# Convolution and GELU feed-forward on one core: five buffers for convolved blocks, first taps on ScalarE, new instruction orders

## The chip, the core and the metric

The kernel runs on one NeuronCore of a Trainium2 chip. The core has five engines with an instruction stream each: TensorE (PE: matmuls; its weight loads are listed as PEld), VectorE (DVE), ScalarE (ACT), GpSimd (POOL) and SyncE (SP), which here only issues DMA transfers. The streams run in their own order and meet in semaphores. The metric is the device time of one execution in microseconds, the median of several runs.

## What is computed

x has 8 sequences of 4096 tokens with 192 features, in eight heads of 24. Each head has seven convolution weights, which are put through a softmax; the convolution is causal (six zeros ahead of each sequence). Its result goes through a feed-forward layer with 2048 hidden units and the exact GELU.

```python
def _attn_ref(x, weight):
    w = weight - np.max(weight, axis=-1, keepdims=True)
    w = np.exp(w)
    w = w / (np.sum(w, axis=-1, keepdims=True) + 1e-09)
    x_pad = np.concatenate([np.zeros((B, K - 1, D)), x], axis=1)
    x_unf = x_pad[:, idx, :].reshape(B, S, K, H, group)
    out = np.einsum('hk,bskhg->bshg', w, x_unf)
    ...
def _moe_ref(x, w_in, w_out):
    h = x @ w_in
    g = 0.5 * h * (1.0 + erf(h * inv_sqrt2))
    return g @ w_out
```

## The kernel before, in words

**Blocks.** The 32768 tokens are cut into two halves of 16384, which lie on the upper and lower 64 partitions. A half is cut into 35 blocks: blocks 0 to 5 of 256 tokens, blocks 6 to 34 of 512 (`WS`). For each block n:

- SyncE loads x into one of three `xin` buffers (`load`, L778; load n waits until block n-3 has been transposed).
- VectorE transposes it into `xT` (t*n* in the lists; L984), and GpSimd copies the six tokens ahead of it (`halo`, L892).
- The convolution has seven taps. The first (`k` = 0 in `tap`, L332) is a multiplication into `acc`; it can be done by VectorE (L340) or, third by third, by ScalarE (`first_tap`, L1118, L1123; written f0.n, f1.n, f2.n). Taps 1 to 6 multiply and add (L345), on VectorE; the last writes the convolved block in bf16 to `xc` (two buffers). Blocks 0 and 1 are convolved by TensorE.
- TensorE multiplies `xc` by w_in (`mm1`, L1258) in 16 slots of 12 matmuls (8 slots in the small blocks); each slot fills one of two PSUM buffers `hp`, which ScalarE empties by a GELU into `gT` (L1165).
- In the same slots TensorE does the second product, mm2, of the block before, so "TensorE's block n" is mm1(n) with mm2(n-1).

**N and S blocks.** For blocks 6 to 33, mm2 comes in two forms. N blocks multiply all of gT (`mm2_t`, L1343). The 18 S blocks (`ST`, L73) use a scheme of the Strassen kind (`mm2_s`, L1392), with fewer matmuls and more additions. VectorE (`st_add`) and the DMA engines (`st_dma`, accumulating transfers issued by GpSimd) form sums of gT: S1, S3, Dn, S4, in pieces such as S1.0.30 (piece 0 of block 30). Each piece must be there before the matmuls that use it. Behind the matmuls, ScalarE copies results out of four PSUM banks (`st_copy`, L743: p15, e, u, p3). GpSimd moves the copy u from the lower to the upper 64 partitions by two DMA transfers (cu into `uu`, cg into `gs`). VectorE combines them (`st_post`: k0 L751, k3 L758, k4 L764) and transposes the results into `osb` (ev.0, ev.1, ev.2; L776, for N blocks L463). k4 waits for cg, k3 for cu. k4, ev.2 and the copies also release PSUM banks to the next block's mm2. SyncE stores `osb` (L806).

**What sets the order.** It is written out by hand for four engines. `LIST[n]` is VectorE's: t is a transposition, a digit is a tap of block n, the rest are sums, k steps, transpositions to osb and, in the new version, w (a step of preparing the weights for mm2) and evac (emptying block 5). Blocks up to 8 have a default order, with w and evac at places given by `SIDE` (L570). `SLOT[n]` is ScalarE's: "5:f1.10" is an operation ahead of the GELU of slot 5 of block n. `GLIST` (L819) is GpSimd's. SyncE's loop (L1468) issues loads up to block n+4, or n+5 from block 8 on, and then store n-1. Every stream is strictly in order; an instruction that waits holds up all behind it.

Of the kernel before, what the change touches and what calls it, by code (L numbers as in the profile page):

```python
# [5 lines left out]
ALU = mybir.AluOpType  # L6
# [5 lines left out]
def bass_lightweight_conv__then__act_gelu_exact_kernel(  # L12
# [39 lines left out]
    NX = 3  # L52

# [22 lines left out]
        9: "ev.0.6 t10 1 2 ev.2.6 ev.1.6 3 4 5 6",  # L76
        10: "1 2 S1.0.8 t11 ev.0.7 3 4 S1.1.8 S1.2.8 ev.1.7 S3.2.8 5 6",
        11: "ev.2.7 Dn.1.8 S4.0.8 S4.1.8 k0.0.8 t12 1 2 3 ev.2.8 4 5 6",
        12: "t13 1 2 k4.0.8 S1.0.10 3 ev.0.9 4 ev.0.8 S1.1.10 k3.0.8 ev.1.8 5 ev.2.9 ev.1.9 S1.2.10 6",
        13: "Dn.1.10 S3.2.10 1 S4.0.10 S4.1.10 2 k0.0.10 S1.0.11 3 4 5 ev.2.10 S1.1.11 Dn.0.11 S1.2.11 Dn.1.11 S3.2.11 t14 6",  # L80
        14: "k4.0.10 0 S4.0.11 S4.1.11 k0.0.11 t15 k3.0.10 1 2 ev.2.11 ev.1.10 ev.0.10 3 4 5 6",
        15: "t16 1 2 S1.0.13 3 ev.0.12 k4.0.11 k3.0.11 S1.1.13 4 ev.1.11 5 ev.0.11 ev.1.12 S1.2.13 6",
        16: "S3.2.13 t17 ev.2.12 Dn.1.13 S4.0.13 S4.1.13 k0.0.13 S1.0.14 1 2 3 ev.2.13 S1.1.14 4 S1.2.14 5 S3.2.14 Dn.0.14 k4.0.13 Dn.1.14 S4.0.14 S4.1.14 k0.0.14 6",
        17: "ev.0.13 0 1 k3.0.13 ev.1.13 2 ev.2.14 3 t18 4 5 6",
        18: "k3.0.14 t19 S1.0.16 1 k4.0.14 2 ev.0.15 3 S1.1.16 4 ev.1.14 ev.0.14 S1.2.16 ev.1.15 ev.2.15 Dn.1.16 S3.2.16 5 6",
        19: "S4.0.16 k0.0.16 S4.1.16 S1.0.17 t20 1 S1.1.17 2 ev.2.16 Dn.0.17 S1.2.17 3 S3.2.17 4 Dn.1.17 k4.0.16 S4.0.17 S4.1.17 5 k0.0.17 k3.0.16 6",
        20: "0 t21 1 ev.2.17 2 ev.0.16 ev.1.16 3 4 k4.0.17 5 k3.0.17 ev.0.17 6",
        21: "S1.0.19 1 ev.0.18 2 t22 S1.1.19 3 ev.1.17 ev.2.18 S1.2.19 ev.1.18 4 Dn.1.19 S3.2.19 5 S4.0.19 S4.1.19 6",
        22: "k0.0.19 S1.0.20 t23 1 2 ev.2.19 S1.1.20 Dn.0.20 S1.2.20 3 S3.2.20 S4.0.20 Dn.1.20 k4.0.19 4 S4.1.20 ev.0.19 k0.0.20 5 6",
        23: "t24 0 k3.0.19 ev.1.19 ev.2.20 1 2 3 4 5 6",  # L90
        24: "t25 S1.0.22 k4.0.20 1 ev.0.21 2 S1.1.22 3 ev.1.21 ev.2.21 S1.2.22 S4.0.22 S3.2.22 k3.0.20 4 Dn.1.22 ev.0.20 ev.1.20 S4.1.22 5 k0.0.22 6",
        25: "1 t26 2 ev.2.22 3 4 5 6",
        26: "1 2 t27 S1.0.24 ev.0.23 3 k4.0.22 S1.1.24 4 k3.0.22 ev.0.22 ev.1.22 ev.1.23 S1.2.24 S3.2.24 5 ev.2.23 6",
        27: "S4.0.24 Dn.1.24 1 S4.1.24 k0.0.24 S1.0.25 t28 2 3 ev.2.24 S1.1.25 4 S1.2.25 Dn.0.25 Dn.1.25 S3.2.25 S4.0.25 k4.0.24 ev.0.24 k3.0.24 5 S4.1.25 k0.0.25 6",
        28: "t29 0 1 ev.1.24 ev.2.25 2 3 4 5 6",
        29: "t30 1 S1.0.27 ev.0.26 k3.0.25 2 S1.1.27 k4.0.25 3 4 S1.2.27 S3.2.27 ev.1.26 ev.1.25 ev.2.26 ev.0.25 S4.0.27 5 Dn.1.27 S4.1.27 6",
        30: "k0.0.27 t31 1 2 3 ev.2.27 4 5 6",
        31: "1 t32 2 k4.0.27 3 k3.0.27 S1.0.29 ev.1.27 ev.0.28 S1.1.29 4 5 ev.1.28 S1.2.29 6",
        32: "ev.0.27 Dn.1.29 S4.0.29 S3.2.29 ev.2.28 1 S4.1.29 2 k0.0.29 S1.0.30 3 t33 4 ev.2.29 Dn.0.30 S1.1.30 S1.2.30 5 6",
        33: "S3.2.30 k3.0.29 k4.0.29 Dn.1.30 S4.0.30 S4.1.30 ev.1.29 ev.0.29 k0.0.30 1 S1.0.31 2 ev.2.30 S1.1.31 3 S1.2.31 t34 S3.2.31 Dn.0.31 4 k4.0.30 Dn.1.31 S4.0.31 S4.1.31 k3.0.30 k0.0.31 5 6",  # L100
        34: "S1.0.32 S1.1.32 1 ev.2.31 ev.0.30 S1.2.32 Dn.0.32 S4.0.32 Dn.1.32 ev.1.30 S3.2.32 k4.0.31 S4.1.32 2 3 k0.0.32 4 5 S1.0.33 k3.0.31 6",
        35: "ev.2.32 S1.1.33 S1.2.33 Dn.0.33 S4.0.33 Dn.1.33 S3.2.33 ev.0.31 ev.1.31 k4.0.32 k3.0.32 ev.0.32 S4.1.33 k0.0.33 ev.1.32 ev.2.33 k4.0.33 ev.0.33 k3.0.33 ev.1.33",
    }
    SLOT = {
        7: "2:f0.9 3:f1.9 5:f2.9",
        8: "3:f0.10 3:f1.10 6:f2.10 13:f0.11",
        9: "5:f1.11 6:p15.8 10:f2.11 13:f0.12 14:e.8",
        10: "0:f1.12 2:u.8 3:p3.8 4:f2.12 6:f0.13 10:f1.13",
        11: "1:f2.13 6:p15.10 13:e.10",
        12: "0:p3.10 2:u.10 6:p15.11 8:f2.14 11:f0.15 13:e.11 14:f1.15",  # L110
        13: "1:p3.11 2:u.11 4:f2.15 11:f0.16",
        14: "1:f1.16 4:f2.16 6:p15.13 9:f2.17 14:e.13",
        15: "0:p3.13 2:u.13 6:p15.14 13:e.14",
        16: "0:u.14 2:p3.14 4:f0.18 6:f1.18 8:f2.18 10:f0.19 13:f1.19",
        17: "7:p15.16 10:f2.19 12:f2.20 14:e.16",
        18: "0:p3.16 2:u.16 6:p15.17 13:e.17",
        19: "0:u.17 2:f0.21 4:p3.17 6:f1.21 8:f2.21",
        20: "5:f0.22 6:p15.19 10:f1.22 10:f2.22 13:e.19 14:f2.23",
        21: "0:p3.19 2:u.19 6:p15.20 13:e.20 15:f0.24",
        22: "2:u.20 4:p3.20 5:f1.24 8:f2.24 11:f0.25",  # L120
        23: "5:f1.25 6:p15.22 10:f2.25 13:e.22 14:f0.26",
        24: "0:u.22 2:p3.22 4:f1.26 4:f2.26 12:f0.27",
        25: "1:f1.27 4:f2.27 6:p15.24 14:e.24",
        26: "0:p3.24 2:u.24 6:p15.25 11:f2.28 13:f0.29 14:e.25",
        27: "0:p3.25 2:f1.29 4:u.25 6:f2.29",
        28: "0:f0.30 2:f1.30 6:p15.27 10:f2.30 13:f0.31 14:e.27",
        29: "0:f1.31 2:f2.31 3:u.27 4:p3.27 8:f0.32 10:f1.32 13:f2.32",
        30: "6:p15.29 14:e.29",
        31: "0:p3.29 2:u.29 4:f0.33 7:p15.30 8:f1.33 9:f2.33 13:e.30",
        32: "0:p3.30 2:u.30 4:f0.34 7:p15.31 9:f1.34 10:f2.34 15:e.31",  # L130
        33: "0:p3.31 2:u.31 6:p15.32 13:e.32",
        34: "0:p3.32 2:u.32 7:p15.33 15:e.33 15:u.33",
# [3 lines left out]
    AT1 = {4: (3, 5, 6), 5: (3, 5, 6), 6: (2, 3, 5)}  # L136
    for n in range(M0 + 3, NB):
        AT1[n] = [(b, i) for b in SLOT for i, k, m in SLOT[b] if k[0] == "f" and m == n]
# [51 lines left out]
    with es:  # L190
# [17 lines left out]
        xc = [sbt("xc%d" % i, [128, NP * TB], BF16) for i in range(2)]  # L208
# [5 lines left out]
        sst = {k: sbt("s_" + k, [128, NF // 2 * TB], BF16) for k in ("S1", "Dn", "S4")}  # L214
        gsm = sbt("gsm", [128, TB], F32)
        p5s = sbt("p5s", [128, TB], F32)
        uu = sbt("uu", [128, TB], F32)
        tq = sbt("tq", [128, TB], F32)
# [45 lines left out]
        S_AD = {k: sem("S_AD" + k) for k in ("S3.0", "S3.1", "S3.2", "Dn.0", "Dn.1", "cp.0", "cp.1", "cu", "cg")}  # L264
# [35 lines left out]
        def conv_out(e, n, j):  # L300
            kd, h, d0, dw = pieces(n)[j]
            p, ex, c0, w = kinds(n)[kd]
            e.wait_ge(S_PC, PCB[n] + kd + 1)
            ro = slice(0, 128) if h is None else slice(64 * h, 64 * h + 64)
            ri = ro if not ex else slice(64 - 64 * h, 128 - 64 * h)
            o = p * TB + c0 + d0
            dst = xc[n % 2][ro, o : o + dw]
            cb = 512 * cbank(n, kd) + d0
            src = ob[ri, cb : cb + dw]
            if (n == 0 and j in PA) or (n, j) == (1, 0):  # L310
                e.activation(out=dst, in_=src, func=AF.Copy).then_inc(S_PCA)
            else:
                e.tensor_copy(dst, src).then_inc(S_PCE)
# [18 lines left out]
        def tap(e, n, k, p0, pn):  # L332
# [9 lines left out]
            if k == KS - 1:  # L342
                dst = ap(xc[n % 2], p0 * TB, [[NP * TB, 128], [TB, pn], [1, w]])
                e.wait_ge(S_MM1, SL0[n - 1])
# [213 lines left out]
        for m in ST:  # L558
            for name in SUMS:
                for q in range(len(SUMS[name]) - 1):  # L560
                    p = "%s.%d" % (name, q)
                    key, one = (p, 16) if p in BYDMA[m] else (name, 1)
                    count[key] = count.get(key, 0) + one
# [947 lines left out]
```

## Time and profile before

| | us |
|---|---|
| median of 3 runs (667.45, 668.77, 668.36) | 668.36 |
| time of the profiled execution | 666.53 |
| its span, first to last instruction | 664.8 |
| VectorE busy | 623.6 |
| of it the convolution's taps 1 to 6 (L345) | 339.0 |
| ScalarE busy | 591.1 |
| of it the GELUs (L1165) | 514.6 |
| of it first taps (L1123), 77 of them | 53.5 |
| GpSimd busy | 105.5 |

The span is one execution, taken by the hardware profiler; what lies around it is 1.7 us. "Busy" is the time in which an engine executes an instruction. A wait row names the engine that waited, the operation it waited with, the engine and operation that ended the wait, the total, the number of times and the longest. In the rows of instruction groups there stand the line, engine, operation, output and input, count, busy time, mean in ns, and the idle time of the engine just ahead of them.

### The profile page before, as it was taken

What the parts mean: (1) busy time and instruction counts of PE and PEld (TensorE: products, weight loads), DVE (VectorE), ACT (ScalarE), POOL (GpSimd) and SP (SyncE); (2) the same over time, 40 slices, a digit from 0 to 9 for tenths busy, and PEclk for the clock granted to TensorE, in tenths of its full rate; (3) what the DMA queues carried; (4) which work ended last, traced back from release to release, by engine and by line L of the source; (5) the groups of instructions that cost most, each with busy time, mean ns of one, the idle gap of its engine ahead of it and who ended that gap; (6) DMA issues with size and microseconds to landing.
All of it is one profiled execution on the core that took longest, in us unless ns stands there. A gap on an engine that the chain in (4) does not pass through costs nothing.

```text
span 664.8 us, 27970 instructions
## 1 busy us (share of the span) xinstructions
PE 658.9 (99%) x12792; PEld 478.9 (72%) x12792; DVE 623.6 (94%) x564; ACT 591.1 (89%) x691; POOL 105.5 (16%) x175
## 2 busy tenths in 40 slices
PE   9999999999999999999999999999999999999997
PEld 8999655576776677778777666757666757677776
DVE  5989999999999999999999999999999999999962
ACT  8899988898899898989889998989898998999882
POOL 8000540102010110202120102110102030111010
DMA  9746675645914691596189145959245838352454
GB/s 156 162 96 133 109 121 122 136 98 130 216 40 113 156 193 34 138 206 124 38 192 221 34 106 120 195 115 225 45 98 136 184 82 192 66 113 50 92 134 112
DMA packets 146438, 83.66 MB, mean 126 GB/s; under 512 B 129936, under 2 KB 138192, under 8 KB 146320
## 3 DMA queue, kind: packets, MB, share of 16 engines
q1 hardware_dynamic: 129328, 49.42, 33.7%
q0 software_dynamic: 15872, 31.86, 23.7%
q8 instruction: 100, 1.64, 1.0%
q10 hardware_dynamic: 1120, 0.59, 0.3%
q14 instruction: 18, 0.15, 0.1%
HBM read 31.51 MB, written 25.17 MB: 85 GB/s over the span
## 4 chain that ended last, share of the span: by engine, by line
PE 94%; DMA 2%; DVE 2%; POOL 1%; issue 1%; ACT 0%; DVEq 0%; POOLq 0%; ACTq 0%
PE hp L1258 48%; PE ob L1392 25%; PE ob L1343 16%; PE ob L1298 4%; DVE acc L345 1%; PE hp L1448 1%; DMA win<-in_moe_w_in_dram 1%; DMA xin<-in_x_dram 1%; PE ob L1448 1%; DMA uu<-uu 0%; ACT gT L1165 0%; POOL win L839 0%; DVE xT L984 0%; POOL xTb L360 0%; DVE xc L345 0%
## 5 line engine op out<-in xcount | busy, mean ns | idle before, releaser
L1165 ACT ACTIVATE gT<-hp 128x1024 bf16<-128x1024 f32 x510 | 514.6, 1022 | 60.1 <-PE hp L1258 52.7
L1258 PE MATMUL hp<-xc,win 64*64 64x512 bf16 (+2 forms) x6036 | 432.6, 366 | 0.5 <-DVE xc L345 0.4
L1258 PEld LDWEIGHTS hp<-xc,win 64*64 64x64 bf16 (+1 forms) x6036 | 229.1, 105 | 88.6 <-ACT gT L1165 5.9
L345 DVE SCALAR_TENSOR_TENSOR acc<-xT,wcol,acc 128x1536 f32<-128x1536 f32 (+1 forms) x165 | 282.3, 1711 | 7.4 <-ACT acc L1123 4.6
L1392 PE MATMUL ob<-gT,wot 64*64 64x512 bf16 x1152 | 219.6, 376 | 0.0
L1392 PE MATMUL ob<-gT,wst 64*64 64x512 bf16 (+2 forms) x1152 | 203.1, 323 | 0.7 <-DVE p5s L764 0.7
L1343 PE MATMUL ob<-gT,wot 64*64 64x512 bf16 x1920 | 133.5, 376 | 0.0
L1392 PE MATMUL ob<-s_S,wot 64*64 64x128 bf16 (+2 forms) x864 | 132.5, 305 | 0.0
L1392 PEld LDWEIGHTS ob<-gT,wst 64*64 64x64 bf16 x1152 | 98.5, 107 | 16.3 <-DVE p5s L764 1.6
L1392 PEld LDWEIGHTS ob<-gT,wot 64*64 64x64 bf16 x1152 | 89.5, 107 | 10.9 <-DVE osb L776 0.5
L1343 PEld LDWEIGHTS ob<-gT,wot 64*64 64x64 bf16 x1920 | 63.9, 107 | 39.7 <-DVE osb L776 0.3
L1392 PEld LDWEIGHTS ob<-s_S,wot 64*64 64x64 bf16 x864 | 68.6, 107 | 15.9
L1392 PE MATMUL ob<-s_Dn,wst 64*64 64x512 bf16 x288 | 79.5, 376 | 0.0
L1392 PE MATMUL ob<-s_S,wst 64*64 64x512 bf16 x288 | 79.5, 376 | 0.0
L671 POOL DMA_DIRECT2D gT<-gT x36 | 32.1, 902 | 198.3 <-DVE s_S L699 198.3
L984 DVE STREAM_TRANSPOSE xT<-xin 128x1536 f32<-128x1536 f32 (+2 forms) x39 | 59.4, 1532 | 3.5 <-DMA xin<-in_x_dram 2.8
L345 DVE SCALAR_TENSOR_TENSOR xc<-xT,wcol,acc 128x1536 bf16<-128x1536 f32 (+1 forms) x33 | 56.7, 1717 | 0.8
L1123 ACT ACTIVATE acc<-xT,wcol 128x512 f32<-128x512 f32 (+1 forms) x77 | 53.5, 698 | 0.0
L699 DVE TENSOR_TENSOR s_S<-gT 128x1024 bf16<-128x1024 bf16 (+1 forms) x54 | 45.8, 853 | 2.6 <-PE ob L1392 1.2
L708 DVE TENSOR_TENSOR s_S<-gT,s_Dn 128x2048 bf16<-128x2048 bf16 x36 | 43.1, 1218 | 0.4
L1298 PE MATMUL ob<-wout,gT 64*128 64x192 bf16 x768 | 42.0, 243 | 0.0
L892 POOL COPY xT<-xT 128x18 f32<-128x18 f32 x29 | 14.9, 514 | 156.8 <-DVE xc L345 145.1
(92 smaller groups left out, 416.1 us busy)
## 6 DMA issues: line engine op xcount, KB each, us to landing
out_dram<-osb SPq DMA_DIRECT2D x124, 192.0 KB, 3.5
xin<-in_x_dram SPq DMA_DIRECT2D x116, 192.0 KB, 4.2
gT<-gT POOLq DMA_DIRECT2D x18, 512.0 KB, 5.1
s_Dn<-gT POOLq DMA_DIRECT2D x9, 512.0 KB, 2.9
gT<-gT POOLq DMA_DIRECT2D x18, 256.0 KB, 4.1
s_Dn<-s_S POOLq DMA_DIRECT2D x9, 512.0 KB, 5.6
uu<-uu POOLq DMA_DIRECT2D x18, 128.0 KB, 2.6
xin<-in_x_dram SPq DMA_DIRECT2D x18, 96.0 KB, 2.5
```

Of the source, the lines that this page charges most:

```text
L345: return e.scalar_tensor_tensor(dst, src, wk, a, op0=ALU.mult, op1=ALU.add)
L671: e.dma_start(quad(m, 1, 0, k, k1 - k), quad(m, 0, 0, k, k1 - k), accum_op=ALU.add).then_inc(S_AD["S3.%d" % q], 16)
L699: ins = v.tensor_tensor(t("S1"), quad(m, 1, 0, k, n), quad(m, 1, 1, k, n), ALU.add)
L708: ins = v.tensor_tensor(t("S4"), quad(m, 0, 1, k, n), t("Dn"), ALU.add)
L892: g.tensor_copy(dst, src).then_inc(S_HALO)
L984: v.transpose(out, src).then_inc(S_TR)
L1123: a.activation(out=acc[n % 2][:, p * TB : p * TB + w], in_=ap(xT[n % 2], p * XW + HX, [[NP * XW, 128], [1, w]]), func=AF.Copy, scale=wcol[ ...
L1165: a.activation(out=ap(gT[n % 2], (i % 2 * NF + i // 2) * TB if n in ST else i * c * 2 * w, dst), in_=ap(ob, 2 * TB, [[4 * TB, 128], *src[1 ...
L1258: ins = t.matmul(hbuf(u, slice(fo, fo + fw), o, w), ap(win, f1, [[NP * F, 64], [2, fw]]), xc[n % 2][r, p * TB : p * TB + w], start=(p == 0 ...
L1298: ins = t.matmul(bb[sub], gT[m % 2][r, c0 : c0 + 128], wout[r, CH[sub][i] * C : (CH[sub][i] + 1) * C], start=(ph == 0 and k == 0), stop=(p ...
L1343: ins = t.matmul(bank(BK[m][j], slice(64 * h, 64 * h + 64), w), ap(wot, 64 * hf * NF * C + CH[h][i] * C + 64 * j, [[NF * C, 64], [1, 64]]) ...
L1392: ins = t.matmul(bank(BK[m][bk], slice(64 * cg, 64 * cg + 64))[:, c0 : c0 + w], wt_, x, start=(e == mine[0]), stop=(e == mine[-1] or e in ...
```

## The change

- `xc` has five buffers instead of two (`NXC`), so the last tap of block n waits for mm1 of block n-5 instead of n-2.
- The first taps of all blocks from 4 on are ScalarE's, all three thirds. Before, VectorE did all of them in blocks 7 and 8 and two thirds in 14, 17, 20, 23 and 28.
- The lower-to-upper copy u has two buffers (`uu`, `u2`), used in turn by S blocks, with semaphores of their own; so the next u need not wait for k3 and cg of the block before, but of the one before that.
- The first half of Dn has two buffers (`s_Dn`, `dn2`) in the same manner.
- VectorE's list starts at block 4 and holds the weight steps and evac, and all lists are in a new order. Loads run ahead by a table `AHEAD`.
- `st_dma` can also form a piece of S1 by DMA; no list uses that. The matmuls of TensorE and their order are the same.

```diff
+    NXC = 5
+    AHEAD = {4: 11, 5: 11, 7: 13, 8: 15, 9: 16, 10: 16, 11: 19, 12: 19, 13: 20, 14: 21, 15: 22, 16: 23, 17: 25, 18: 25, 19: 25, 22: 26, 23: 31, 24: 31, 25: 33, 26: 33, 27: 33, 28: 35, 29: 35}
...
     LIST = {
+        4: "t5 w.0.0 w.1.0 1 2 w.2.0 3 4 5 6",
+        5: "t6 1 2 3 4 w.3.0 5 6",
+        6: "w.4.0 t7 1 w.5.0 2 w.6.0 3 4 5 6",
+        7: "t8 1 2 3 evac.0.5 w.7.0 4 5 6",
+        8: "evac.1.5 t9 1 2 3 4 5 6",
-        9: "ev.0.6 t10 1 2 ev.2.6 ev.1.6 3 4 5 6",
-        10: "1 2 S1.0.8 t11 ev.0.7 3 4 S1.1.8 S1.2.8 ev.1.7 S3.2.8 5 6",
+        9: "ev.0.6 1 t10 2 ev.2.6 3 ev.1.6 4 5 w.8.0 6",
+        10: "t11 1 2 S1.0.8 3 S1.1.8 ev.0.7 w.9.0 4 ev.1.7 S1.2.8 ev.2.7 Dn.1.8 S3.2.8 5 6",
...
-        12: "t13 1 2 k4.0.8 S1.0.10 3 ev.0.9 4 ev.0.8 S1.1.10 k3.0.8 ev.1.8 5 ev.2.9 ev.1.9 S1.2.10 6",
+        12: "t13 1 2 3 S1.0.10 4 ev.0.9 k4.0.8 k3.0.8 S1.1.10 5 ev.1.8 ev.0.8 ev.1.9 S1.2.10 S3.2.10 6",
...
-        26: "1 2 t27 S1.0.24 ev.0.23 3 k4.0.22 S1.1.24 4 k3.0.22 ev.0.22 ev.1.22 ev.1.23 S1.2.24 S3.2.24 5 ev.2.23 6",
+        26: "1 2 k4.0.22 t27 ev.0.23 3 ev.0.22 S1.0.24 4 S1.1.24 5 ev.1.23 S1.2.24 Dn.1.24 S3.2.24 k3.0.22 ev.2.23 ev.1.22 6",
...
-        32: "ev.0.27 Dn.1.29 S4.0.29 S3.2.29 ev.2.28 1 S4.1.29 2 k0.0.29 S1.0.30 3 t33 4 ev.2.29 Dn.0.30 S1.1.30 S1.2.30 5 6",
-        33: "S3.2.30 k3.0.29 k4.0.29 Dn.1.30 S4.0.30 S4.1.30 ev.1.29 ev.0.29 k0.0.30 1 S1.0.31 2 ev.2.30 S1.1.31 3 S1.2.31 t34 S3.2.31 Dn.0.31 4 k4.0.30 Dn.1.31 S4.0.31 S4.1.31 k3.0.30 k0.0.31 5 6",
-        34: "S1.0.32 S1.1.32 1 ev.2.31 ev.0.30 S1.2.32 Dn.0.32 S4.0.32 Dn.1.32 ev.1.30 S3.2.32 k4.0.31 S4.1.32 2 3 k0.0.32 4 5 S1.0.33 k3.0.31 6",
+        32: "S1.2.29 ev.2.28 ev.1.28 ev.1.27 S3.2.29 S4.0.29 ev.0.27 Dn.1.29 1 S4.1.29 k0.0.29 2 S1.0.30 3 t33 S1.1.30 ev.2.29 4 Dn.0.30 S1.2.30 S3.2.30 S4.0.30 5 Dn.1.30 k4.0.29 S4.1.30 k3.0.29 ev.1.29 k0.0.30 ev.0.29 6",
+        33: "t34 S1.0.31 S1.1.31 1 ev.2.30 2 S1.2.31 Dn.0.31 Dn.1.31 S3.2.31 S4.0.31 S4.1.31 k4.0.30 3 4 k3.0.30 k0.0.31 5 6",
+        34: "S1.0.32 S1.1.32 Dn.0.32 ev.2.31 1 ev.1.30 S1.2.32 S4.0.32 S3.2.32 ev.0.30 Dn.1.32 k4.0.31 2 S4.1.32 3 k0.0.32 4 5 S1.0.33 6",
...
     SLOT = {
...
-        8: "3:f0.10 3:f1.10 6:f2.10 13:f0.11",
-        10: "0:f1.12 2:u.8 3:p3.8 4:f2.12 6:f0.13 10:f1.13",
+        4: "2:f1.6 5:f2.6 6:f0.7",
+        7: "0:f0.8 3:f1.8 3:f2.8 8:f0.9 9:f1.9 12:f2.9",
+        8: "1:f0.10 5:f1.10 6:f2.10 10:f0.11 10:f1.11",
+        10: "0:u.8 2:p3.8 3:f2.12 5:f0.13 9:f1.13",
...
-        30: "6:p15.29 14:e.29",
-        31: "0:p3.29 2:u.29 4:f0.33 7:p15.30 8:f1.33 9:f2.33 13:e.30",
-        34: "0:p3.32 2:u.32 7:p15.33 15:e.33 15:u.33",
+        30: "1:f1.32 3:f2.32 7:p15.29 13:e.29",
+        31: "0:p3.29 2:u.29 4:f0.33 6:p15.30 10:f1.33 10:f2.33 13:e.30 14:f0.34",
+        34: "0:p3.32 2:u.32 7:p15.33 13:e.33 15:u.33",
...
-    AT1 = {4: (3, 5, 6), 5: (3, 5, 6), 6: (2, 3, 5)}
-    for n in range(M0 + 3, NB):
+    AT1 = {}
+    for n in range(4, NB):
...
-        xc = [sbt("xc%d" % i, [128, NP * TB], BF16) for i in range(2)]
+        xc = [sbt("xc%d" % i, [128, NP * TB], BF16) for i in range(NXC)]
+        dn2 = sbt("dn2", [128, NF // 4 * TB], BF16)
+        u2 = sbt("u2", [128, TB], F32)
...
-                e.wait_ge(S_MM1, SL0[n - 1])
+                if n >= NXC:
+                    e.wait_ge(S_MM1, SL0[n - NXC + 1])
...
+        def sums(m, name, k, n, r=slice(0, 128), c0=0):
+            if name == "Dn" and k < NF // 4 and ST.index(m) % 2:
+                return dn2[r, k * TB + c0 :][:, :n]
+            return sst[name][r, k * TB + c0 :][:, :n]
...
+        def us(m):
+            return (uu, u2)[ST.index(m) % 2]
...
         GLIST = (
...
-            "cu.0.27 cp.0.29 S3.0.29 S3.1.29 Dn.0.29 halo.33 S3.0.30 S3.1.30 cu.0.29 "
-            "cg.0.29 S3.0.31 S3.1.31 cg.0.30 cu.0.30 halo.34 S3.0.32 S3.1.32 cg.0.31 "
+            "halo.32 cp.0.29 S3.0.29 Dn.0.29 S3.1.29 S3.0.30 halo.33 S3.1.30 cg.0.29 "
+            "cu.0.29 S3.0.31 S3.1.31 cg.0.30 cu.0.30 S3.0.32 halo.34 S3.1.32 cg.0.31 "
...
-                while xs < min(NB, n + 5 + (1 if n >= 8 else 0)):
+                while xs < min(NB, AHEAD.get(n, n + 5)):
```

## The prediction

> **What bounds the kernel now.** I read the page's busy times first, then the windows of 20 us, then who waited for whom, then the chain of waits where the windows show a hole.
>
> ```profile
> PE 658.9 (99%) x12792; PEld 478.9 (72%) x12792; DVE 623.6 (94%) x564; ACT 591.1 (89%) x691; POOL 105.5 (16%) x175
> PE 94%; DMA 2%; DVE 2%; POOL 1%; issue 1%; ACT 0%; DVEq 0%; POOLq 0%; ACTq 0%
> ```
>
> TensorE is busy 99% of the span and is 94% of the chain that ended last. Nothing in this diff takes a matmul away, so the change can win only idle time of TensorE. Where is any left?
>
> ```profile
> 0.00:20.00 20.00, 18.75 (x394) 17.63 (x396) 12.11 (x34) 16.97 (x27) 13.60 (x30) 1.00 0.87 143
> 20.00:40.00 20.00, 19.59 (x418) 19.40 (x414) 19.44 (x21) 17.66 (x23) 1.37 (x2) 1.00 0.62 150
> ...
> 560.00:580.00 20.00, 19.28 (x392) 13.34 (x387) 18.79 (x17) 17.36 (x22) 2.82 (x4) 1.00 0.53 108
> ```
>
> The first figure after the length is TensorE's. Between 40 and 640 us every window has 20.00, save 560 to 580. But a busy TensorE hides short stalls, so I also measured the pace of the matmuls. Starts of four 64x64x512 matmuls are 216 ns apart in the steady state; giving each matmul its share of that, I looked for the places behind which the starts never catch up. They are: +0.92 us at 578.3, +0.16 at 583.5, +0.11 at 193.6, +0.14 at 630.3, +0.74 and +0.22 at 650.8 and 652.0, and nothing else above 0.06. A second reading agrees: counting 192 matmuls of L1258 to a block, blocks begin 20.72 us apart where the one before is N and 19.87 where it is S, and the block that starts at 569.4 takes 20.83 instead of 19.87. Over blocks 7 to 33 the excess is 1.75 us in all. That is the ceiling, 0.26% of the time.
>
> ```profile
> PEld ob L1392 <- DVE p5s L764: 1.6, 2, 1.2
> ...
> 571.43 0.85 POOL gT L671
> 572.28 1.28 issue
> 573.56 0.01 POOLq L664
> 573.57 3.27 DMA uu<-uu
> 576.85 0.02 issue
> 576.87 0.32 DVE wtf L758
> ...
> 577.54 0.70 DVE p5s L764
> ...
> 578.28 0.74 PE ob L1392 x10
> ```
>
> This is the one large stall. TensorE waits for p5s at L764, which is k4.0.29. VectorE has it behind k3.0.29 (L758), which waits 1.08 us for the DMA cu.0.29; that took 3.27 us, and GpSimd issued it ahead of cg.0.29 (the DMA that k4 needs), at 573.57 and 574.16. TensorE wanted k4 at 578.28 - 0.92 = 577.36.
>
> VectorE is the second bound. From the last convolution step of each block to TensorE's first matmul of that block the lead is 1.2 us at block 3, 1.7 and 1.9 at 6 and 7, then 5 to 17, and at the end 3.65 at block 33 and 0.15 at block 34.
>
> **The change, part by part.**
>
> *First taps to ScalarE.*
>
> ```profile
> L340 DVE TENSOR_SCALAR acc<-xT,wcol 128x1024 f32<-128x1024 f32 x7 | 5.2, 740 | 0.0
> L1123 ACT ACTIVATE acc<-xT,wcol 128x512 f32<-128x512 f32 x71 | 50.5, 715 | 0.0
> ACT gT L1165 <- PE hp L1258: 52.7, 177, 0.7
> ```
>
> Blocks 7, 8, 14, 17, 20, 23 and 28 lose L340: 7 x 0.74 + 2 x 0.49 = 6.2 us off VectorE. ScalarE gains 7 x 2 + 2 = 16 taps. One occupies it 0.61 us (the tap at 86.73, the next gelu at 87.34), so 9.8 us. Its 52.7 us of waiting for matmuls cover that. The cover has a limit in one place: a gelu may start about 0.85 us late before TensorE lacks its half of hp (1.97 us from one matmul group to the next use of its buffer, less 1.12 for the gelu). One tap costs 0.61, two in one slot 1.22, less some 0.3 us of idle. Three slots have two taps before; after, seven have two taps and one a tap with a copy. None of the three shows a stall above 0.03; the arithmetic allows up to 0.1. Bounds for five more: 0 to 0.5 us; I take 0.1, near the rows seen.
>
> *Five buffers for xc.* VectorE waited 0.8 us in 33 final taps (the xc row at L345), and its lead is below one block, so two buffers were not what held it. Nothing gained; nothing lost.
>
> *Two buffers for U, two for the first half of Dn.* ScalarE's u waited 0.6 us once, for TensorE at the tail. Nothing by itself. Without it the copy of the next u would wait for k3, which the new order puts later.
>
> *SyncE's loads further ahead.* A load waits for a transposition, and stores stand behind it. From the new lists, load 10 (behind t7) stands before store 3, load 30 (behind t27) before store 22, whose last transposition ev.1.22 comes after t27 in the same list. So the waits keep VectorE's order. VectorE waited for xin once, 2.8 us, before 20 us. Cost nothing; without that cover a late store would delay ev.2, which releases a PSUM bank.
>
> *Weight steps and list order, early.* I laid VectorE's new list along the rows of the old trace (convolution tap 1.85 us behind another, 1.73 before something else; transposition 1.69). Convolution 6 ends at 66.3 (66.2 before; TensorE wants it at 67.87). Then three new waits appear. evac.0.5 stands ahead of three taps of block 7, and half of block 6's matmuls end at 75.8: 2.4 us lost. evac.1.5 waits for 83.6: 1.4 us. Block 8's taps wait for ScalarE's two taps in slot 3 of block 7, done about 89.3: 3.4 us. Behind these stand convolutions 7 and 8, ending at 82.3 (wanted 83.62) and 100.3 (wanted 104.36). So 7.2 us of idle against 6.2 saved. Convolution 9 ends at 114.8, 1.2 later than now, with 10 us of lead. The last weight step w.9.0 ends at 124.5; TensorE needs it at 125.7. All hidden, by 1.2 us at least.
>
> *Around block 31.* cg.0.29 now goes before cu.0.29: issued at 573.57, and p5s<-uu takes a median of 2.2 us to land, so 575.8 to 576.8 (upper end: the 3.27 that cu took). k4.0.29 moves ahead of k3, behind S1.2.30, S3.2.30, S4.0.30, a tap and Dn.1.30. From k0.0.29 (P7 done at 560.1) these add up to 577.15 for its end. It is wanted at 577.36. So the 0.92 us go, with 0.2 in hand, or 0.2 remains if the DMA takes the longer time.
>
> *The end.* k3.0.31 (0.74 us) moves behind the last tap of block 34, and VectorE's idle 1.08 us at 576 is filled, so the 0.14 at 630.3 goes, and the 0.16 at 583.5 with it. At 650.8 TensorE waited for ev.2.33, behind e.33 in slot 15 of ScalarE; e.33 moves to slot 13. But u.33 stays in slot 15: it waits for the last matmul of mm2(33), runs 650.48 to 650.97, and the last gelu behind it ends at 651.97. TensorE then only waits at its thirteenth matmul instead of its first. Nothing gained there.
>
> **Sum**, against the profiled execution's 666.53 (span 664.8 and 1.7 around it): -0.92 - 0.16 - 0.14 + 0.1 = -1.1, so 665.4. The 0.11 at 193.6 stays: the same operations stand before it. The median of the runs, 668.36, lies 1.83 above the profiled time; I leave that as it is: 667.2. The runs differ by 1.3 us among themselves, which I can't place; work that now ends just in time may share in it, so I take 667.1.
>
> A rule that would change the price of a failure: granted clock is 1.00 in every window, and no wait of TensorE in mid-kernel is above 0.92 us. The Trainium skill, page "TensorE: Matmul & The Clock Gate", section "Part 1: The HAM clock gate", says an idle window of about 3.4 us halves the clock until about 3.4 us of work have passed; by it a stall that long would cost an estimated 1.7 us more. No run here shows it.
>
> **Rivals.**
>
> *The stall stays (nothing measurable).* VectorE reaches k4.0.29 later than 577.36, since five more operations stand ahead of it. For: only 0.2 us in hand by my ledger. Against: VectorE saves 3.7 us of first taps behind block 9. Then only 0.3 of the 1.2 us is won: 668.1.
>
> *ScalarE's taps wait for a transposition (slower).* ScalarE runs its taps in order with the gelus. f0.13 stands in slot 5 of block 10 (about 152.3), and t13 ends at 151.5 by my ledger: 0.8 us in hand. Each microsecond that VectorE runs later beyond that stops gelu and then TensorE. For: 7.2 us of new idle early on, and leads of 1.3 us at blocks 6 and 7. Against: in the trace no tap ever waited (0.0 idle at L1123). It turns the sign when VectorE is 0.8 + 1.2 = 2.0 us behind my ledger; at 4 us the price is 3.2 - 1.2 = +2.0: 670.4.
>
> *More comes back than the profile shows.* The runs lie 0.9 to 2.2 us above the profiled execution. If that is the same just-in-time work, the whole 1.75 and some 0.8 of this go: 665.8.
>
> **How the numbers follow.** About 0.2% (1.3 us) is what a measurement of this kernel can tell from no change. Forecast near 667.1: 0.50, cut by that line, 0.28 below it and 0.22 above. Stall stays: 0.10, no difference. More: 0.16, faster. Taps wait: 0.24, slower. So faster 0.44, same 0.32, slower 0.24. Range: 665.7, the case "more" with the whole spread, to 669.9, a VectorE 3.5 us late. The forecast's own range is 666.4 to 668.0.
>
> **What would show it.** Right: no wait of TensorE for L764's successor near 577; blocks 7 to 33 with under 0.8 us of excess; VectorE idle 2 us at 73 to 76 and 3 us before 89; L340 only in blocks 2 and 3. Wrong: idle time of ScalarE before a first tap, with TensorE waiting for gT within the next slots; TensorE waiting at 125.7 for the weights; a wait for k4 that remains. A gain above 2.5 us would say that the ceiling was misread.

## The result and the profile after

| | before | after |
|---|---|---|
| median of 20 runs each, taken together | 667.12 us (665.98 to 668.77) | 666.23 us (665.22 to 667.98) |
| ratio of the times, 95% interval | 1 | 0.9986 (0.998 to 0.9993) |
| profiled execution: time, span | 666.53, 664.8 us | 665.89, 664.2 us |

The change makes the kernel 0.14% faster, 0.93 us by the ratio. The interval leaves 1 out, and the gain is below the 0.2% that the prediction named as its line. The three runs that the table of the kernel before lists have a median 1.2 us above the one that 20 runs gave.

The page of the kernel after, busy times and the chain that ended last:

```profile
PE 658.3 (99%) x12792; PEld 505.6 (76%) x12792; DVE 619.1 (93%) x555; ACT 598.3 (90%) x707; POOL 106.7 (16%) x175
...
PE 96%; DMA 2%; ACT 1%; DVE 0%; issue 0%; POOL 0%; ACTq 0%; DVEq 0%
```

VectorE's busy time fell by 4.5 us and ScalarE's rose by 7.2. (Added up instruction by instruction, VectorE's work fell by 6.4 us, as the first taps let expect; neighbouring instructions overlap a little, and busy time counts an overlap once.) TensorE was busy 99% of the span and is so still. VectorE's share of the chain fell from 2% to under half a percent, and ScalarE's rose to 1%.

Windows of the kernel after (length; then TensorE, weight loads, VectorE, ScalarE, GpSimd, each with its instructions in brackets; granted clock; DMA share; GB/s):

```profile
60.00:80.00 20.00, 20.00 (x344) 15.70 (x341) 17.57 (x12) 19.55 (x23) 6.88 (x13) 1.00 0.50 95
80.00:100.00 20.00, 20.00 (x362) 11.10 (x362) 15.05 (x10) 18.88 (x22) 6.83 (x13) 1.00 0.84 138
...
560.00:580.00 20.00, 19.50 (x396) 15.67 (x391) 18.84 (x18) 17.50 (x22) 3.46 (x5) 1.00 0.43 94
```

VectorE now idles 2.4 us between 60 and 80 and 5.0 between 80 and 100, and TensorE shows nothing of it. Between 560 and 580 TensorE has 19.50 instead of 19.28: the hole has become smaller and is still there. Who waited for whom, after (total, times, longest, in us):

```profile
DVE p5s L803 <- DMA p5s<-u: 6.3, 2, 5.3
DVE acc L359 <- ACT acc L1157: 5.4, 4, 3.5
...
DVE osb L438 <- PE ob L1332: 3.4, 2, 2.1
...
PEld ob L1426 <- DVE p5s L803: 1.3, 2, 1.0
```

The second and third rows are the early waits: block 8's taps behind ScalarE's (3.5 us the longest) and the two evac steps. The last row is what is left of the wait that was 1.6 before. The chain of waits of the kernel after at that place (start, length, what), and below it VectorE's own timeline (start, length; in brackets the idle time before, and what ended it):

```profile
572.87 0.48 ACT u L782
...
573.64 3.65 DMA p5s<-u
...
577.38 0.70 DVE p5s L803
...
578.12 0.85 PE ob L1426 x12
```

```profile
575.20 1.22 DVE L740 TENSOR_TENSOR s_Dn<-gT,s_S 128x2048 bf16<-128x2048 bf16 x1
577.38 0.69 DVE L803 TENSOR_TENSOR p5s<-ob,p5s 128x512 f32<-128x512 f32 x1 [0.96 <-DMA p5s<-u]
```

k4.0.29 (now L803) has k3 no longer ahead of it. VectorE was there at 576.4 and waited 0.96 us for cg.0.29 itself, which took 3.65 us to land. By the pace of the matmuls 0.70 us of the 0.92 remain.

The pace of the matmuls for the whole execution, in us (excess over matmuls that follow each other without a gap; the last column is the time from the start of the last matmul to the end of the span):

| profiled execution | first 60 us | 60 to 640 | 640 to last matmul | behind it | span |
|---|---|---|---|---|---|
| before | 5.87 | 2.15 | 1.17 | 3.28 | 664.8 |
| after | 5.79 | 1.87 | 1.16 | 3.02 | 664.2 |
| after, a second one (e10) | 5.47 | 1.63 | 1.18 | 3.06 | 663.7 |

So 0.3 to 0.5 us came out of the stages that the change rearranges. By the prediction's own count, 216 ns for four matmuls, the 60-to-640 column would read 1.75 before and 1.47 after; the differences are the same. The 0.2 behind the last matmul is a single store: in these three executions the last to land is the one that ScalarE issues when it has copied out the last matmuls, and it landed 2.24 us after its issue before, 1.97 and 2.01 us after. No edit is aimed at that, so it isn't shown to be the change's. The first column is not the change's: over all executions here it lies between 5.27 and 5.89, and a kernel (e4) whose program differs from before only from block 31 on has 5.29.

### The profile page after: what moved, and what is told of

It reads as the page before. It is cut to its first block, busy times and chain, and to the rows that moved or that the text cites. A ratio compares the mean times of both kernels' runs of the same rounds, so it can differ in the third digit from the quotient of the medians.

```text
span 664.2 us, 27974 instructions
## 1 busy us (share of the span) xinstructions
PE 658.3 (99%) x12792; PEld 505.6 (76%) x12792; DVE 619.1 (93%) x555; ACT 598.3 (90%) x707; POOL 106.7 (16%) x175
## 3 DMA queue, kind: packets, MB, share of 16 engines
q8 instruction: 100, 1.64, 1.1%
## 4 chain that ended last, share of the span: by engine, by line
PE 96%; DMA 2%; ACT 1%; DVE 0%; issue 0%; POOL 0%; ACTq 0%; DVEq 0%
PE hp L1292 49%; PE ob L1426 25%; PE ob L1377 16%; PE ob L1332 5%; DMA win<-in_moe_w_in_dram 1%; PE hp L1482 1%; PE ob L1482 1%; DMA p5s<-u 1%; ACT gT L1199 0%; DMA wsb<-in_weight_dram 0%; DVE wcol L996 0%; POOL win L381 0%; DVE p5s L803 0%; POOL win L878 0%; POOL dg L901 0%
## 5 line engine op out<-in xcount | busy, mean ns | idle before, releaser
L1292 PE MATMUL hp<-xc,win 64*64 64x512 bf16 (+2 forms) x6036 | 438.6, 366 | 0.6 <-DVE win L381 0.5
L1292 PEld LDWEIGHTS hp<-xc,win 64*64 64x64 bf16 (+1 forms) x6036 | 241.8, 105 | 75.9 <-ACT gT L1199 7.3
L1426 PE MATMUL ob<-s_S,wot 64*64 64x512 bf16 (+2 forms) x864 | 132.7, 305 | 0.0
L1377 PEld LDWEIGHTS ob<-gT,wot 64*64 64x64 bf16 x1920 | 71.0, 107 | 32.6
L1426 PEld LDWEIGHTS ob<-gT,wot 64*64 64x64 bf16 x1152 | 88.9, 107 | 8.6
L1157 ACT ACTIVATE acc<-xT,wcol 128x512 f32<-128x512 f32 (+1 forms) x93 | 64.6, 702 | 0.0
L1426 PE MATMUL ob<-s_Dn,wst 64*64 64x512 bf16 x216 | 61.0, 376 | 0.0
L1332 PEld LDWEIGHTS ob<-wout,gT 64*128 64x128 bf16 x768 | 35.1, 94 | 3.3
L1426 PEld LDWEIGHTS ob<-s_S,wst 64*64 64x64 bf16 x288 | 30.8, 107 | 4.4
```

The costliest lines, as they stand in the source:

```text
L1157: a.activation(out=acc[n % 2][:, p * TB : p * TB + w], in_=ap(xT[n % 2], p * XW + HX, [[NP * XW, 128], [1, w]]), func=AF.Copy, scale=wcol[ ...
L1292: ins = t.matmul(hbuf(u, slice(fo, fo + fw), o, w), ap(win, f1, [[NP * F, 64], [2, fw]]), xc[n % NXC][r, p * TB : p * TB + w], start=(p == ...
L1332: ins = t.matmul(bb[sub], gT[m % 2][r, c0 : c0 + 128], wout[r, CH[sub][i] * C : (CH[sub][i] + 1) * C], start=(ph == 0 and k == 0), stop=(p ...
L1377: ins = t.matmul(bank(BK[m][j], slice(64 * h, 64 * h + 64), w), ap(wot, 64 * hf * NF * C + CH[h][i] * C + 64 * j, [[NF * C, 64], [1, 64]]) ...
L1426: ins = t.matmul(bank(BK[m][bk], slice(64 * cg, 64 * cg + 64))[:, c0 : c0 + w], wt_, x, start=(e == mine[0]), stop=(e == mine[-1] or e in ...
```

## The experiments

Ratios are to runs of the kernel before on the same chip (its medians were 667.15 us beside e1 to e4, 667.12 beside e5 to e8, 666.85 beside e9 and e10). Excess means the 60-to-640 column of the table above, place by place where a time is given.

**e1, the copy of U one slot earlier.** Its DMA starts earlier, so k4 should be in time.

```diff
-        31: "0:p3.29 2:u.29 4:f0.33
+        31: "0:p3.29 1:u.29 4:f0.33
```

> The changed kernel with one entry moved: the copy u.29 of ScalarE stands ahead of the GELU of slot 1 of block 31 instead of slot 2, some 1.2 us earlier. Theory A (the stall of 0.70 us that is left at 578 is the DMA cg.0.29 alone: issued at 573.64 behind u.29, landed at 577.29): cg is issued near 572.4 and lands by 576.1, k4.0.29 follows Dn.1.30 at 576.4 and ends near 577.1, TensorE's stall there falls from 0.70 to under 0.15, the span from 664.2 to about 663.6, the ratio to the kernel before to about 0.9977. Rival B (VectorE would be late at k4.0.29 anyway): the stall stays at 0.5 or more, ratio 0.9986 as the changed kernel's.

666.23 us, ratio 0.999 (0.9981 to 0.9999). cg.0.29 was issued at 573.05 and landed 2.19 us later; the 0.70 at 578 is gone. The chain of waits of e1:

```profile
570.63 0.08 ACT wtf L782
...
571.25 1.02 ACT gT L1199
572.27 0.47 ACT u L782
572.75 0.92 ACT gT L1199
...
573.71 0.84 PE hp L1292 x12
```

In its place stands a late gelu: p3 and u now lie one slot apart, each 0.6 us on ScalarE, and TensorE loses 0.25 us at 573.71. The trace is 0.45 better at this place; the time can't be told from after's. The cause of the remaining stall is shown: with an early landing it is gone. The other kernels with after's order agree: the stall is absent where cg.0.29 lands in 2.19 us (e1, e3, e8), and is 0.41 us for 3.38 (e6), 0.51 for 3.45 and 3.46 (e2, e7), 0.57 for 3.52 (e10), 0.67 for 3.62 (e5) and 0.70 for 3.65 (after).

**e2, the tail.** u.33 goes behind the last gelu of block 34, so that TensorE need not wait for that gelu at 651.64.

```diff
-        34: "0:p3.32 2:u.32 7:p15.33 13:e.33 15:u.33",
-        35: "0:p3.33",
+        34: "0:p3.32 2:u.32 7:p15.33 13:e.33",
+        35: "0:u.33 0:p3.33",
```

> The changed kernel with the copy u.33 moved from ahead of the last GELU (slot 15 of block 34) to behind it. Theory A (the waits of 0.25 and 0.67 us near 650 and 651.6 are the last GELU, held up by u.33): the last GELU starts near 649.6 instead of 650.58, TensorE's thirteenth matmul of the last product no longer waits, and the end comes 0.6 to 0.7 us sooner: ratio to the kernel before about 0.9976. Rival B (the end hangs on the stores and the bank releases): no change, 0.9986.

666.25 us, ratio 0.9992 (0.998 to 1.0003); span 664.8. The 0.67 at 651.64 is gone, and the end is not earlier for it. SyncE's queue, after and then e2:

```profile
656.47 2.60 SPq L845 DMA_DIRECT2D out_dram<-osb  x4
659.12 2.57 SPq L459 DMA_DIRECT2D out_dram<-osb  x4
```

```profile
657.42 2.35 SPq L845 DMA_DIRECT2D out_dram<-osb  x4
659.81 2.94 SPq L459 DMA_DIRECT2D out_dram<-osb  x4
```

The last stores (L459) stand behind those of block 33 (L845), and these wait for u.33, its DMA, k3.0.33 and a transposition. u.33 came later, so all of that did: the last stores were issued by 662.75 instead of 661.69, and the last matmul at 661.02 instead of 661.14 bought nothing. Some 0.55 us of this lateness is not the edit's: the execution had already lost 0.56 us at 353.9, where nothing was edited (last section). Counted from the start of the last matmul, the end comes 3.77 us later instead of 3.02, and that takes back the 0.68 won at the tail; e8, with the same edit, has 3.94. What lands last has changed. In the kernel after it is ScalarE's store behind the last matmul, at 663.75, with SyncE's last at 663.24; in e2 it is SyncE's, at 664.38, with ScalarE's at 663.61. So moving u.33 can't win the stall at the tail, because the stores move with it.

**e3, both, and u one slot earlier in all nine places where an S block follows an S block.** The edit is that of e1 in blocks 12, 15, 18, 21, 26, 31, 32, 33 and 34, with that of e2.

> Both edits together, and u one slot earlier in all nine places where one S block follows another (u.10, u.13, u.16, u.19, u.24, u.29, u.30, u.31, u.32). Theory A: 0.6 at block 31, 0.65 at the end and some 0.1 to 0.2 us of the small waits near 193, 310, 598 are gone: 1.4 us, ratio to the kernel before about 0.9965. Rival B: an earlier u puts two copies into neighbouring slots and delays GELUs, so waits of TensorE for gT come up; then under half of it is won, 0.998 or more.

668.18 us, ratio 1.0021 (1.0011 to 1.003): slower. Gelus are late by about 0.25 us at 189.3, 250.1, 372.3, 575.1, 595.3, 615.5 and 635.7 and by 0.1 elsewhere; 0.53 at 354.3 is of another kind (last section). At these places, with p3 and u in neighbouring slots, ScalarE bears the first copy and TensorE pays for part of the second. That is no rule for every slot: the kernel after has first taps in neighbouring slots (8 and 9 of block 12) and two in one slot (10 of block 21), and TensorE loses about 0.1 us at most there.

**e4, the local edits of block 31 and the end, alone, in the kernel before.** cg.0.29 ahead of cu.0.29, k4.0.29 ahead of k3.0.29, k3.0.31 behind the last tap of block 34.

```diff
-        ... S3.1.30 cu.0.29 cg.0.29 S3.0.31
+        ... S3.1.30 cg.0.29 cu.0.29 S3.0.31
-        33: "S3.2.30 k3.0.29 k4.0.29 Dn.1.30
+        33: "S3.2.30 k4.0.29 k3.0.29 Dn.1.30
-        34: "... S1.0.33 k3.0.31 6",
-        35: "ev.2.32 S1.1.33 S1.2.33 Dn.0.33
+        34: "... S1.0.33 6",
+        35: "ev.2.32 S1.1.33 S1.2.33 k3.0.31 Dn.0.33
```

> The kernel before with three entries moved and nothing else: cg.0.29 ahead of cu.0.29 in GpSimd's list, k4.0.29 ahead of k3.0.29 in VectorE's, and k3.0.31 behind the last tap of block 34. Theory A (the change gains by these few places, not by buffers and first taps): the stalls of 0.92 and 0.14 us shrink, by 0.3 to 0.9 us in all, ratio to the kernel before 0.9987 to 0.9996. Rival B (the gain comes from VectorE's 6.2 us of first taps and the order as a whole): ratio 0.9997 or more.

667.49 us, ratio 1.0005 (0.9996 to 1.0013): nothing. The chain of waits of e4 shows why:

```profile
573.09 3.69 DMA p5s<-uu
...
576.87 0.70 DVE p5s L764
...
577.62 0.85 PE ob L1392 x12
```

The swap makes cg the first of the two copies, and now it is cg that lands after 3.69 us. 0.75 us remain there, and 0.25, 0.46 and 0.32 us stand at 580, 583.7 and 638.5, where the kernel before had 0.16 at 583.5. The stall at 630 went, as foreseen. So this run tests the three edits with a late landing, as the kernel after had it, and not with an early one.

**e5, the first taps of five blocks given back to VectorE in the kernel after.**

```diff
-        14: "k4.0.10 t15
+        14: "k4.0.10 0 t15
-        28: "1 t29 2
+        28: "0 1 t29 2
-        26: "0:p3.24 2:u.24 4:f0.28 6:p15.25 10:f1.28 10:f2.28
+        26: "0:p3.24 2:u.24 6:p15.25 10:f2.28
```

and so in blocks 17, 20 and 23.

> The kernel after with the first taps of blocks 14, 17, 20, 23 and 28 two thirds back on VectorE (5 x 0.74 = 3.7 us) and 10 taps of 0.61 us off ScalarE; all else as after. VectorE idles 6.0 us between 100 and 640 us in the kernel after, all of it in waits for other engines. Theory A, the saved first taps are what pays: VectorE has no room of its own, the last convolution step of block 34 (0.60 us ahead of TensorE now) comes 1 to 3 us later and TensorE waits there: ratio to before 1.000 to 1.003. Theory B, the new order pays and VectorE's waits shrink by what it is given back: ratio 0.998 to 0.9995, TensorE's excess as in the kernel after.

667.15 us, ratio 0.9999 (0.999 to 1.0009): the gain is gone as far as runs can tell (the interval of the kernel after, 0.998 to 0.9993, just overlaps this one). Excess is 3.06 instead of 1.87. Theory A was right in the time and wrong in the place: the lead at block 34 is 0.67 us, against 0.60 in after. The price fell due at 197.1 (0.71 us, a sum late) and at 490.2 (0.63 us). The chain of waits of e5 before the second:

```profile
481.69 1.73 DVE xc L359
483.42 0.68 DVE acc L353
...
487.64 1.78 DVE acc L359
...
489.45 0.73 DVE osb L815
...
490.23 0.84 PE ob L1377 x12
```

L353 is the tap that was given back, 0.68 us; L815 is a transposition behind which a PSUM bank comes free, and it is late by 0.63. The stalls at 583.5 and 630.3 stay away; both losses stand at places that had none before. What VectorE saves here is not a lead at the next convolution but the punctuality of the sums and releases between its taps.

**e6, two buffers for xc in the kernel after.**

```diff
-    NXC = 5
+    NXC = 2
```

> The kernel after with two convolved buffers in place of five. Theory A, the buffers do nothing but allow the order: the largest lead of VectorE over TensorE is 18.8 us (block 31), just below a block of 19.9 to 20.7 us, so a final tap waits for at most some tenths: ratio to before 0.998 to 0.9995, VectorE's final taps waiting under 1 us in all. Theory B, the buffers carry the gain: VectorE's final taps wait for TensorE's last matmul of the block before, over 2 us in all, and stalls return behind 580: ratio 1.000 or above.

666.24 us, ratio 0.999 (0.998 to 1.0001). VectorE waited once in a final tap, 0.58 us until 549.30. The trace has about 0.25 us of small excess at 552.7, 553.0 and 571.9 that after lacks; the median is after's to 0.01 us. Five buffers do nothing that can be measured.

**e7, the last weight step one tap later in the kernel after.**

```diff
-        10: "t11 1 2 S1.0.8 3 S1.1.8 ev.0.7 w.9.0 4 ev.1.7
+        10: "t11 1 2 S1.0.8 3 S1.1.8 ev.0.7 4 w.9.0 ev.1.7
```

> The kernel after with the last weight step w.9.0 moved behind tap 4 in block 10's list. By the ledger it then ends 1.8 us later, at 126.3, and TensorE needs it at 125.7: a wait of about 0.6 us there. Theory A, the ledger's margin of 1.2 us is real and a stall there costs its length: the trace shows 0.4 to 0.8 us of TensorE at 125.7, and the time is up by as much, ratio to before 0.9990 to 1.0000. Theory B, the margin is larger than the ledger says, or a stall so early is caught up by work that waits later: no stall, or a stall and the time of the kernel after, 0.9986.

The chain of waits of e7:

```profile
123.93 1.70 DVE acc L359
125.63 0.35 DVE wst L656
...
126.03 0.84 PE ob L1426 x10
```

The step ended at 125.98 and TensorE waited for it: 0.73 us at 126.03, within the 0.4 to 0.8 expected. The stall is there; the time is 666.91 us, ratio 0.9999 (0.9984 to 1.0013), too wide to tell whether all of it was paid. The profiled execution also lost 0.54 us at 354.3, where nothing was edited (last section).

**e8, u.29 and p3.29 exchanged, and the tail of e2.**

```diff
-        31: "0:p3.29 2:u.29 4:f0.33
+        31: "0:u.29 2:p3.29 4:f0.33
```

> The kernel after with u.29 and p3.29 exchanged on ScalarE in block 31 (u two slots earlier, no two copies in neighbouring slots) and u.33 behind the last gelu. Theory A: the DMA that k4.0.29 waits for is issued about 571.5, the 0.70 us at 578 and the 0.67 us at 651.6 go, and no gelu is late: excess of blocks 7 to 33 under 0.7 us, ratio to before 0.996 to 0.998. Theory B: u in slot 0 waits for its matmuls or p3 late holds a bank, a gelu is late by 0.2 to 0.5 us, and other transfers that land late take what is left: 0.998 to 0.9995, as in the first two runs.

666.63 us, ratio 0.9989 (0.9979 to 0.9999). cg.0.29 was issued at 571.74 and landed in 2.19 us; the stall at 578 is gone. But p3 now empties its half of a bank two slots later, and TensorE waits for that. Waits of e8 between 573 and 575:

```profile
PEld ob L1426 <- ACT wtf L782: 0.7, 1, 0.7
```

That is 0.41 us of excess at 574.0. Another 0.33 us arose at 353.8, where nothing was edited. The chain of waits of e8 there:

```profile
339.88 4.35 DMA gsm<-uu
...
344.32 0.70 DVE gsm L803
...
349.62 4.16 DMA gT<-gT
...
353.82 0.62 PE ob L1426 x7
```

cg.0.19, another of the small copies, took 4.35 us to land; in the kernel after it took 2.85, without a stall. Theory B.

**e9, the offload alone: the kernel before, lists in their old order, five blocks' first taps on ScalarE.** Each of lists 14, 17, 20, 23 and 28 loses its tap 0, and ScalarE's slots get f0 and f1 of these blocks behind their transposition, for example

```diff
-        14: "1:f1.16 4:f2.16 6:p15.13 9:f2.17 14:e.13",
+        14: "1:f1.16 4:f2.16 6:p15.13 9:f0.17 10:f1.17 11:f2.17 14:e.13",
```

> The kernel before, its lists of VectorE in their old order, with the first taps of blocks 14, 17, 20, 23 and 28 all on ScalarE (5 x 0.74 = 3.7 us off VectorE, 10 taps of 0.61 us more on ScalarE). Theory A, VectorE's time behind block 9 is what pays, in whatever order: ratio to before 0.998 to 0.9993, the 0.16 at 583.5 and the 0.12 at 630.3 smaller or gone. Theory B, the taps pay only with lists made for them: VectorE idles by what it is given, since what it comes to early is not ready, and the 0.92 at 578 stays behind cu.0.29: ratio 0.9993 to 1.0005, TensorE's excess within 0.3 us of before.

668.31 us, ratio 1.0017 (1.0006 to 1.0028): slower. VectorE's waits between 100 and 640 us add up to 9.7 us, against 4.9 in the kernel before: 4.8 more, where it was given 3.7. Its lead at block 34 stayed at 0.15. ScalarE's timeline of e9 where three taps lie in neighbouring slots:

```profile
237.09 1.02 ACT L1165 ACTIVATE gT<-hp 128x1024 bf16<-128x1024 f32 x1 [0.28 <-PE hp L1258]
238.01 0.71 ACT L1123 ACTIVATE acc<-xT,wcol 128x512 f32<-128x512 f32 x1
238.62 1.01 ACT L1165 ACTIVATE gT<-hp 128x1024 bf16<-128x1024 f32 x1
...
241.05 0.72 ACT L1123 ACTIVATE acc<-xT,wcol 128x512 f32<-128x512 f32 x1
241.66 1.94 ACT L1165 ACTIVATE gT<-hp 128x1024 bf16<-128x1024 f32 x2
```

Gelus follow 1.52 us apart where TensorE makes one ready in about 1.3, and TensorE loses 0.23 us at 242.74. Five such places sum to 0.97 us (0.16, 0.23, 0.12, 0.15, 0.31). At 579.9 the old stall is 1.50 instead of 0.92: cu.0.29 took 3.85 us to land instead of 3.27. Theory B, and worse than it said. These slots were chosen too close together, and that part of the loss is this kernel's own, not the offload's; the later landing isn't the offload's either, as far as is known. What the same taps would be worth in the old lists with slots further apart, nothing or a little, no run shows.

**e10, the kernel after once more.**

> The kernel after, unchanged, for a second profiled execution. Theory A, the time at which the small copies of U land varies between executions of one program, and TensorE's stalls with it: cg.0.29 (issued about 573.6) lands after 2.2 to 4 us, the stall at 578 is between 0 and 1.0 us; cg.0.19 lands after 2.8 to 4.6 us, and a stall of 0 to 0.5 us at 353.8 comes with a landing above 4. Theory B, the landings are fixed by the program: 3.65 us and 2.85 us again, 0.70 at 578 and none at 353.8. The ratio to before is 0.998 to 0.9993 by both.

665.95 us, ratio 0.9983 (0.9972 to 0.9993), beside 0.9986 the first time. cg.0.29 took 3.52 us (3.65), the stall at 578 is 0.57 (0.70); cg.0.19 took 3.27 (2.85), no stall at 353.8 either time. The landings do vary between executions of one program, here by 0.13 and 0.42 us. Theory B's exact numbers are missed by that much. Theory A's ranges hold, but they are wide, and neither landing was late enough to show the stall at 353.8; so this run alone says little of how far a landing can stray.

## Why the prediction was right, and where not

*Time and range.* 667.1 us was forecast, 666.23 measured, inside the range. As a change it was -1.26 us from the 668.36 of the three runs; by the ratio it is -0.93 (-0.47 to -1.33). The forecast called "faster by over 0.2%" its likeliest class, and the ratio lies just on the other side of that line. The level is in part luck: 666.23 lies just below the narrower range of 666.4 to 668.0 that the prediction gave for its own forecast, and it is as low as that because the level it started from, 668.36, was 1.24 us above the median of 20 runs, and not because more was won. Of the signs it named, VectorE's early waits and L340 (now L353) in blocks 2 and 3 alone came as said. An excess under 0.8 us did not: it is 1.47 between 60 and 640 us. And a wait for k4 remains, which it had listed as a sign of being wrong.

*The ceiling, right.* Only TensorE's idle time could be won, 1.75 us over blocks 7 to 33; no run here gained more than that.

*The term at block 31, mis-sized.* The prediction took 0.92 us off, with cg.0.29 landing after 2.2 us, at most 3.27. It landed after 3.65, and 0.22 us came off instead of 0.92. Its ledger for VectorE was right: Dn.1.30 ended at 576.4, so with an early landing k4 would have ended at 577.1 (0.70 later), in time for 577.36. The caution "or 0.2 remains if the DMA takes the longer time" named the cause and under-priced it, because its upper end was one observation from the same spot. e4 shows the same copy at 3.69 in the old order; e1 shows the stall gone when the copy landed in 2.19.

*The small stalls, right.* 0.16 at 583.5 and 0.14 at 630.3 are gone. The 0.11 at 193.6, said to stay, has become three pieces of 0.06, 0.07 and 0.04 around 193.5 to 196.4. New ones of 0.05 to 0.09 stand at 309.9, 598.1 and 613.3, where the prediction's 0.1 for ScalarE's fuller slots had allowed for as much; no slot with two taps shows one.

*The early ledger, right to some tenths.* Convolutions 6, 7, 8 and 9 ended at 66.41, 82.41, 100.48 and 114.76 (forecast 66.3, 82.3, 100.3, 114.8). The waits foreseen as 2.4 and 1.4 us for evac are 3.4 together by the row above; 3.4 for block 8's taps is 3.5. The margin of the last weight step, 1.2 us, is 1.1 by e7: 1.85 us later cost 0.73.

*First taps, a term left out.* They take 6.2 us off VectorE. Giving 3.7 us of them back in e5 costs 1.2 us of excess and, by the medians, the whole gain. The prediction had counted them at nothing of their own, and put the gain on single edits. e4 (three of the edits without the taps) gives nothing, e5 (the lists without five blocks' taps) gives nothing, e9 (those taps without the lists) is slower, in part by its choice of slots. Place by place, the new order removes the stalls at 583.5 and 630.3 and the taps keep it from costing more at other places. So the gain needs taps and lists together; that much the runs support, though e4 had a late landing and e9 crowded slots.

*Buffers, right.* xc at nothing: e6. The second buffers for U and for the first half of Dn were not tried alone, and neither were the loads further ahead nor the early part of VectorE's list.

*The end, half right.* Nothing was gained at 650 in TensorE, as said (0.92 us of excess there against 0.96). Not foreseen: the time behind the last matmul's start fell by 0.26, because ScalarE's last store landed in 1.97 us instead of 2.24. Block 33's stores were issued 0.65 us earlier (656.47 against 657.12), but some 0.36 of that is what all stages before had gained, and in both kernels SyncE's stores land before ScalarE's last one. e2 shows that they come to be the last when u.33 is moved.

*Rivals.* "The stall stays" described block 31 well, for another reason: VectorE was in time, the DMA was not. "ScalarE's taps wait for a transposition" did not come: ScalarE's taps have 0.0 us of idle time before them, as before. "More comes back" was wrong: it asked for 2.55 us, and 0.93 came; its 665.8 lies near the measured level only because the level before was too high.

*The clock.* Granted clock is 1.00 in every window of the kernel after shown here, and no mid-kernel stall there is above 0.70 us. What the Trainium skill, page "TensorE: Matmul & The Clock Gate", section "Part 1: The HAM clock gate", says of stalls of 3.4 us still can't be seen here; the longest mid-kernel stall of any run, 1.50 us in e9, leaves no lower clock behind it either.

No variant here is faster than the kernel after beyond its interval.

## What to carry to other kernels

When one engine is busy 99% and a second 93%, work taken off the second may need an order made for it before it pays: the same 3.7 us were worth about the whole gain in the new lists and came with a loss in the old ones, in part because of crowded slots. Price a wait for a small DMA by the whole spread of its landings (here 2.2 to 3.7 us at block 31, 2.9 to 4.6 at block 21), not by its median, or issue it that much earlier. And before clearing a stall at the end of a kernel, look at everything that the edit delays: here moving one copy made a queue of stores land last, which had landed before.

## What was not expected of the hardware

**A copy of 128 KB within the chip's SBUF lands after anything from 2.17 us to over 4.** Over the two copies of U in the first six profiled executions (before, after, e1 to e4):

| under way in the copy's first 2.2 us | copies | median, us | over 3 us |
|---|---|---|---|
| no load or store to speak of, no instruction packet | 78 | 2.24 | 9 |
| an instruction packet | 93 | 2.65 | 29 |
| over 50 packets of loads or stores, no instruction packet | 17 | 2.66 | 7 |
| over 50 packets of loads or stores, and an instruction packet | 28 | 4.37 | 21 |

These two are not all. In the first row 38 copies had another transfer of GpSimd's (a piece of a sum, as a rule) under way in the same 2.2 us, and 8 of the 9 late ones are among these, up to 7.8 us; in the second row it is 21 copies, 15 of them late. Of 112 copies in these two rows without any such transfer, 15 took over 3 us.

The page lists a queue for instructions, 100 packets of 16 KB; the table counts this queue. DMA of the kernel after between 573 and 578 us, in 40 slices of 0.125 us (busy tenths, then GB/s), and its queues:

```profile
DMA  0000000000008098992039988000100000000000
GB/s 0 0 0 0 0 0 0 0 0 0 0 0 131 0 295 197 197 229 66 0 98 295 229 197 197 0 0 0 33 0 33 0 33 0 0 0 0 0 0 0
...
q0 software_dynamic: 96, 0.26, 22.5%
q8 instruction: 1, 0.02, 2.0%
```

The two copies, cg and cu, are the 96 packets of q0 and the only other work is one instruction packet, which ran from 574.50 for 1.6 us. By 576.4, 90 of the 96 packets were done; then single packets follow (the three 33s at 576.5, 576.9 and 577.0), each starting where the one before ended, and cg counts as landed at 577.29. The same pattern, one packet of 1.3 to 1.6 us and then a few stragglers, is in e5, e6, e7 and e10, where cg took 3.38 to 3.62. In e8 the copies were done before the packet started, and there are no stragglers. In e1 cg's packets were done about when the instruction packet started, and cu's were not: cg landed in 2.19 us and cu in 4.05, with two stragglers. That the stragglers stood behind the instruction packet on one of the 16 DMA engines fits all of these; the trace doesn't name the engine, and no run took the packet away, so it is argued and not shown.

The Trainium skill, page "Runtime: NRT & Kernel Launch", section "Instruction fetch mechanics", says that each engine's sequencer fetches its instructions over a DMA queue of its own in blocks of 16 KiB, at a cost that is mostly hidden. The packets agree in size (1.64 MB in 100 packets); hidden from the engine that fetches is not hidden from the copies that run beside it, if the reading above holds.

**Such landings make stalls at places that nobody edited.** cg.0.19 landed after 2.85, 3.27, 4.04, 4.35 and 4.56 us in after, e10, e1, e8 and e2, and the excess at 353 to 354 was 0, 0, 0.10, 0.43 and 0.62 us; it took 4.53 and 4.59 in e7 and e3, with about 0.6 us. In e6 it took 4.51 and the excess was only 0.10: there the large DMA behind it in the chain (gT<-gT) landed in 3.69 us, against 4.16 in e1, e2, e3, e7 and e8, so that one has a part too. One profiled execution may show half a microsecond that the next does not have.
